# Two layers of a feed-forward network: the second one in six units of 1004 tokens, its second product two steps behind

## The chip, the cores and the metric

The kernel runs on one core of a Trainium2 chip. Its time is the device time of one execution in microseconds; three runs are shown, and one more execution was taken with the hardware profiler. Engines are called by the names of the profile: PE is TensorE (PEld its weight loads), ACT is ScalarE, DVE is VectorE, POOL is GpSimd, SP is the engine that issues most DMAs.

## The reference

```python
X = np.fft.fft(np.fft.fft(x, axis=1), axis=2).real      # x: 2 x 3008 x 256
x = X.reshape(6016, 256)
h = x @ w_in                                            # first layer, 256 -> 2048
g = where(h >= 1, h, where(h <= -1, 0, (h + 1)**2 / 4))
x = g @ w_out                                           # 2048 -> 256
h = x @ w2_in                                           # second layer, 256 -> 2048
g = maximum(0.01 * h, h)
out = g @ w2_out                                        # 2048 -> 256
```

All inputs and the output are float32 in value; the weights arrive as 64-bit words.

## The kernel before, in words

A first stage (up to about 75 us) makes the Fourier transform in the layout that the layers need, and folds part of it into the first layer's weights. Then come two layers, and the change is in the second. Tokens lie in the columns of a matmul. A layer handles its 6016 tokens in `NU` = 8 units of `UT` = 752, each unit as two halves of `H4` = 376 columns, and the 2048 hidden values as `NF` = 16 blocks of 128. One unit with one block is a step, so a layer has `N1` = 128 steps; the loop over `n` at the end of the function counts the steps of both layers.

Each operand of a matmul is held as a high part and a low part in a rounded float32 type (`FR`), and each product is made as high times high, high times low and low times high. A step of the second layer goes so:

- `first_2(u, f)` (L559): 12 matmuls on PE into `q`, one PSUM tile of two banks (pool `ps_ab`, two such tiles), two halves by two parts of the input by three products.
- L666, ACT writes `s` = 0.01 `q`; L667, DVE writes `s` = max(`q`, `s`).
- one step later `high` (L577): ACT rounds `s` into `gh`; `low` (L581): POOL writes `gl` = `s` - `gh`.
- `LAG` = 4 steps later `second` (L572): 12 matmuls of `gh`, `gl` with the output weights, into four PSUM accumulators `acc` (pool `ps_acc`, four tiles) that stay open for the 16 steps of a unit.
- after the sixteenth block `store` copies the accumulators out, two on ACT (L592) and two on DVE (L593); in the second layer SP then issues two DMAs to `out` (L596). In the first layer the copy is the input `yt[u]` of the second.

PE's order in a step is `first_2` of this step, then `second` of the step four before. Each engine runs its instructions in the order in which this loop issues them. `split_y` (L601 on ACT, L602 on DVE) splits a unit's input into `yh` some steps before the unit begins. The first layer's step (`layer_1`) has the same `high`, `low` and `second`, but only six matmuls in its first product and more elementwise work.

The tiles of both layers come from the same pools: `t3` (3 buffers each of `gh` and `gl`) and `t5` (5 buffers of the first result). Pools `ta`, `th` and `cp` on the right side serve the first layer alone. `jobs` is a list by step of work that is planned in by hand behind a step: the second layer's weights are read, turned to float32 and split from step `N1` - 6 on (`first_weights`, `second_weights`: a DMA, two ACT instructions, three DVE instructions, of which L217 and L222 read two operands from SBUF, and the split).

Of the kernel before, what the change touches and what calls it, by code (L numbers as in the profile page):

```python
# [19 lines left out]
P = 128  # L20
# [5 lines left out]
NU = NT // UT  # L26

# [130 lines left out]
def fnet_moe_kernel(ctx: ExitStack, tc: tile.TileContext, xpq, dft_e, dft_o, dft_d, sgn,  # L158
# [122 lines left out]
    with tc.manual_schedule():  # L281
# [249 lines left out]
        t3 = pool("t3", 3)  # L531
        t5 = pool("t5", 5)
        yp = [pool("yp0", 2)]
        only1 = ExitStack()
        ta = pool("ta", 2, only1, "right")
        th = pool("th", 3, only1, "right")

        N1 = NU * NF
        LAG = 4
# [12 lines left out]
        def first_2(u, f):  # L552
            p = psum_pair(f"q{u}_{f}")
            w, y = wa[f // 2][:, f % 2], yh[u]
            for t in range(2):
                a = 0
                for d in range(2):
                    for x, z in ((0, 0), (0, 1), (1, 0)):
                        T.matmul(p[:, t, :H4], lhsT=w[:, 2 * d + x, :], rhs=y[d][:, z, t, :],  # L559
                                 start=(a == 0), stop=(a == 5))  # L560
                        a += 1
            return p

        def second(n, f):
            if f == 0:
                for k in range(4):
                    acc[k] = psum_one(f"acc{n}_{k}")
            w, a, b = wb[f // 2][:, f % 2], gh.pop(n), gl.pop(n)
            for k in range(4):
                m, t = divmod(k, 2)  # L570
                for i, (x, y) in enumerate(((0, a), (0, b), (1, a))):
                    T.matmul(acc[k][:, :H4], lhsT=w[:, x, m * P:(m + 1) * P], rhs=y[:, t, :],  # L572
                             start=(f == 0 and i == 0), stop=(f == NF - 1 and i == 2))

        def high(n):
            gh[n] = t3.tile([P, 2, H4], FR, tag="gh", name="gh")
            A.copy(gh[n], gp[n])  # L577

        def low(n):
            gl[n] = t3.tile([P, 2, H4], FR, tag="gl", name="gl")  # L580
            G.tensor_tensor(out=gl[n], in0=gp.pop(n), in1=gh[n].bitcast(F32), op=ALU.subtract)  # L581

        def store(n, first):

            u = n % N1 // NF
            if first:
                yt[u] = by.tile([P, 2, 2, H4], F32, tag="by", name=f"y{u}")
                dst = [yt[u][:, m] for m in range(2)]
            else:
                dst = [to.tile([P, 2, H4], F32, tag="o", name=f"o{u}{m}") for m in range(2)]  # L590
            for t in range(2):
                A.copy(dst[0][:, t], acc[t][:, :H4])  # L592
                V.tensor_copy(dst[1][:, t], acc[2 + t][:, :H4])  # L593
            if not first:
                for m in range(2):
                    nc.sync.dma_start(out=out[m, :, u * UT:(u + 1) * UT],  # L596
                                      in_=dst[m].rearrange("p t n -> p (t n)"))

        def split_y(u, d):
            y = yp[u % 2].tile([P, 2, 2, H4], FR, tag="yh", name=f"yh{u}{d}")  # L600
            A.copy(y[:, 0], yt[u][:, d])  # L601
            V.tensor_tensor(out=y[:, 1], in0=yt[u][:, d], in1=y[:, 0].bitcast(F32), op=ALU.subtract)  # L602
            yh.setdefault(u, {})[d] = y
# [16 lines left out]
        for j in range(8):  # L620
            plan_at(20 + 12 * j, *zip((0, 2, 3, 6, 9), w3s[j]))
            plan_at(N1 - 6 + 2 * j, *zip((0, 3, 3), w3s[j][5:]))
            plan_at(N1 - 3 + 2 * j, *zip((0, 1, 2, 2, 3, 4, 4), w4s[j]))
        for d in range(2):
            plan_at(N1 - 26 + 6 * d, (0, lambda d=d: split_y(0, d)))
        for u in range(1, NU):
            plan(N1 + NF * (u - 1) + 8, [lambda u=u: split_y(u, 0)])
            plan(N1 + NF * (u - 1) + 11, [lambda u=u: split_y(u, 1)])

        def layer_1(n):  # L630
# [26 lines left out]
            if new:  # L657
                A.activation(r, r, AF.Square, scale=0.5 / 15.5, bias=0.5)  # L658
                sums(n)

        def layer_2(n):
            if n < 2 * N1:
                u, f = divmod(n - N1, NF)
                p = first_2(u, f)[:, :, :H4]
                gp[n] = g = t5.tile([P, 2, H4], F32, tag="r", name="s")
                A.activation(g, p, AF.Copy, scale=0.01)  # L666
                V.tensor_tensor(out=g, in0=p, in1=g, op=ALU.max)  # L667
            if N1 <= n - 1 < 2 * N1:
                high(n - 1)
                low(n - 1)  # L670
            sums(n)

        def sums(n):
            m = n - LAG
            if m >= 0:
                second(m, m % NF)
                if m % NF == NF - 1:
                    store(m, m < N1)

        for n in range(2 * N1 + LAG):  # L680
            if n < N1:
                layer_1(n)
            else:
                if n < N1 + 2:
                    layer_1(n)
                if n == N1 + 1:
                    only1.close()
                    right.close()
                    yp.append(pool("yp1", 2))
                    to = pool("to", 2)  # L690
                layer_2(n)
            for job in jobs.get(n, ()):
# [49 lines left out]
```

## Time and profile before

| | |
|---|---|
| three runs | 1040.7, 1040.75, 1043.45 us; median 1040.75 |
| the profiled execution | 1040.43 us, span 1038.7 us, so 1.73 us lie outside the span |
| granted TensorE clock, mean over the span | 0.993 |
| PE busy, PEld busy | 1004.1 us (97%), 971.7 us (94%) |
| DVE, ACT, POOL busy | 619.7 us, 624.1 us, 495.6 us |
| first matmul of the second layer | 499.25 us into the span |

A matmul's busy time is longer than the distance to the next one's start, since matmuls overlap; distances between starts are what the text below uses. A granted clock of 1.00 is 2.4 GHz. In a timeline row, "x12" merges twelve like instructions, and the brackets say how long the engine was idle before the row and what released it.

### The profile page before, as it was taken

Reading aid. Unit: us, or ns where it says so; the run is one execution under the profiler, and the core shown is the slowest. Engines: PE = TensorE matmul, PEld = TensorE weight load, DVE = VectorE, ACT = ScalarE, POOL = GpSimd, SP = SyncE. Lnnn points to the kernel's source line nnn. Section 1 sums busy time; section 2 is a strip of 40 time slices with the busy share of each in tenths; the row PEclk is TensorE's granted clock in tenths of the full one; section 3 lists DMA queues with packets and bytes.
Section 4 is the critical chain, followed back from the end, with each engine's and each line's share of the span. In section 5 each row is a group of like instructions: output and inputs, shape, how many; then the busy total and the mean of one; then the engine's idle time right before and its main releaser. Section 6 shows DMA issues by size and latency. Waiting matters only on the chain.

```text
span 1038.7 us, 14411 instructions
## 1 busy us (share of the span) xinstructions
PE 1004.1 (97%) x5656; PEld 971.7 (94%) x5656; DVE 619.7 (60%) x912; ACT 624.1 (60%) x973; POOL 495.6 (48%) x274
## 2 busy tenths in 40 slices
PE   7996879999999999999999999999999999999998
PEld 5656779999999999999999999999999999999998
DVE  5978998898888888897898232232323223233221
ACT  4468678888888788878775444444444444344432
POOL 1004565655565565555644444444444444444443
PEclk9998999999999999999999999999999999999999
DMA  9921000000000000010220000000000000000000
GB/s 298 349 69 41 21 0 2 31 31 1 31 31 2 31 32 1 31 62 2 72 101 21 30 2 1 31 1 30 1 1 31 1 31 1 1 30 1 30 1 31
DMA packets 12164, 39.24 MB, mean 38 GB/s; under 512 B 1472, under 2 KB 1472, under 8 KB 11840
## 3 DMA queue, kind: packets, MB, share of 16 engines
q1 hardware_dynamic: 11232, 35.18, 9.4%
q0 software_dynamic: 864, 3.15, 1.7%
q8 instruction: 44, 0.72, 0.3%
q14 instruction: 24, 0.20, 0.1%
HBM read 30.06 MB, written 8.26 MB: 37 GB/s over the span
## 4 chain that ended last, share of the span: by engine, by line
PE 78%; DVE 9%; ACT 7%; issue 3%; DMA 2%; POOL 0%; DVEq 0%; ACTq 0%; POOLq 0%; SPq 0%
PE acc L572 43%; PE q L559 24%; PE p L548 9%; DVE r L654 2%; ACT gh L577 2%; DMA rw<-in_w_dram 2%; ACT r L658 1%; DVE cw L222 1%; DVE tw L217 1%; DVE aa L641 1%; ACT r L647 1%; DVE h L644 1%; ACT r L651 1%; PE do L442 1%; DMA x<-in_xpq_dram 1%
## 5 line engine op out<-in xcount | busy, mean ns | idle before, releaser
L581 POOL TENSOR_TENSOR gl<-s,gh 128x752 fp32r<-128x752 f32 x128 | 234.0, 1828 | 287.9 <-ACT gh L577 287.9
L581 POOL TENSOR_TENSOR gl<-r,gh 128x752 fp32r<-128x752 f32 x128 | 242.4, 1895 | 175.9 <-ACT gh L577 135.3
L667 DVE TENSOR_TENSOR s<-q,s 128x752 f32<-128x752 f32 x128 | 120.2, 939 | 301.4 <-ACT s L666 301.2
L572 PE MATMUL acc<-gh,wb 128*128 128x376 f32 x1024 | 282.4, 336 | 2.5 <-POOL wb L275 1.3
L559 PE MATMUL q<-yh,wc 128*128 128x376 f32 x1536 | 283.8, 333 | 0.0
L572 PE MATMUL acc<-gh,wd 128*128 128x376 f32 x1024 | 278.7, 333 | 0.6 <-DVE y L593 0.6
L559 PEld LDWEIGHTS q<-yh,wc 128*128 128x128 f32 x1536 | 265.0, 188 | 0.0
L577 ACT CAST gh<-s 128x752 fp32r<-128x752 f32 x128 | 105.1, 821 | 158.2 <-PE acc L572 155.1
L572 PEld LDWEIGHTS acc<-gh,wb 128*128 128x128 f32 x1024 | 187.1, 189 | 6.1 <-ACT r L651 1.8
L572 PEld LDWEIGHTS acc<-gh,wd 128*128 128x128 f32 x1024 | 186.1, 188 | 0.9 <-DVE y L593 0.9
L572 PE MATMUL acc<-gl,wb 128*128 128x376 f32 x512 | 172.6, 337 | 10.9 <-POOL gl L581 10.8
L666 ACT ACTIVATE s<-q 128x752 f32<-128x752 f32 x128 | 102.3, 799 | 124.9 <-PE q L559 124.9
L572 PE MATMUL acc<-gl,wd 128*128 128x376 f32 x512 | 170.5, 333 | 0.0
L548 PE MATMUL p<-bt,wa 127*128 127x376 f32 (+3 forms) x768 | 156.5, 340 | 8.0 <-DVE h L645 4.2
L548 PEld LDWEIGHTS p<-bt,wa 128*128 128x128 f32 (+1 forms) x768 | 136.5, 191 | 10.5 <-issue 5.0
L654 DVE TENSOR_TENSOR r<-h,r 128x752 f32<-128x752 f32 x128 | 129.3, 1010 | 4.5 <-ACT r L658 4.4
L572 PEld LDWEIGHTS acc<-gl,wb 128*128 128x128 f32 x512 | 96.6, 189 | 15.4 <-POOL gl L581 15.4
L647 ACT ACTIVATE r<-h 128x376 f32<-128x376 f32 x128 | 66.1, 517 | 73.7 <-DVE h L644 69.6
L658 ACT ACTIVATE r<-r 128x752 f32<-128x752 f32 x128 | 106.8, 834 | 4.1
L577 ACT CAST gh<-r 128x752 fp32r<-128x752 f32 x128 | 103.2, 806 | 0.1
L641 DVE SCALAR_TENSOR_TENSOR aa<-ct,g,p 128x376 f32<-128x376 f32 (+1 forms) x128 | 77.2, 603 | 41.0 <-PE p L548 40.7
L572 PEld LDWEIGHTS acc<-gl,wd 128*128 128x128 f32 x512 | 96.1, 188 | 0.0
(70 smaller groups left out, 650.6 us busy)
## 6 DMA issues: line engine op xcount, KB each, us to landing
rw<-in_w_dram SPq DMA_DIRECT2D x32, 512.0 KB, 3.7
out_dram<-o SPq DMA_DIRECT2D x16, 376.0 KB, 2.4
x<-in_xpq_dram SPq DMA_DIRECT2D x6, 512.0 KB, 6.4
x<-in_xpq_dram POOLq DMA_DIRECT2D x6, 512.0 KB, 7.7
me<-in_dft_e_dram SPq DMA_DIRECT2D x4, 567.0 KB, 16.0
mo<-in_dft_o_dram SPq DMA_DIRECT2D x2, 1128.0 KB, 19.8
w3f<-cw SPq DMA_DIRECT2D x8, 256.0 KB, 2.2
rf<-w3f SPq DMA_DIRECT2D x8, 256.0 KB, 2.6
```

Of the source, the lines that this page charges most:

```text
L217: V.scalar_tensor_tensor(out=self.tmp, in0=self.high, scalar=-0x80000000, in1=self.tmp, op0=ALU.bitwise_and, op1=ALU.bitwise_or)
L548: T.matmul(p[:, j, :n], lhsT=w[:m, 2 * j + x, :], rhs=b[:m, 2 * j + y, :n], start=(a == 0), stop=(a == 2))
L559: T.matmul(p[:, t, :H4], lhsT=w[:, 2 * d + x, :], rhs=y[d][:, z, t, :], start=(a == 0), stop=(a == 5))
L572: T.matmul(acc[k][:, :H4], lhsT=w[:, x, m * P:(m + 1) * P], rhs=y[:, t, :], start=(f == 0 and i == 0), stop=(f == NF - 1 and i == 2))
L577: A.copy(gh[n], gp[n])
L581: G.tensor_tensor(out=gl[n], in0=gp.pop(n), in1=gh[n].bitcast(F32), op=ALU.subtract)
L641: V.scalar_tensor_tensor(out=aa[:, :w], in0=ct[u][:, :w], scalar=g128[:, f:f + 1], in1=p[:, 0, :w], op0=ALU.mult, op1=ALU.add)
L647: A.activation(r[:, 0], h[:, 0], CLAMP, scale=15.5)
L654: V.tensor_tensor(out=g, in0=hp.pop(n - 1), in1=g, op=ALU.max)
L658: A.activation(r, r, AF.Square, scale=0.5 / 15.5, bias=0.5)
L666: A.activation(g, p, AF.Copy, scale=0.01)
L667: V.tensor_tensor(out=g, in0=p, in1=g, op=ALU.max)
```

## The change

The second layer is cut anew: `NV` = 6 units of two halves of `H6` = 502 columns (the last one of two halves of 498), so 96 steps instead of 128. Its matmuls are as many in a step as before, each over 502 columns. The second layer has its own tiles, `s` (3 buffers, pool `ts`), `gh2` and `gl2` (2 buffers each, pool `g2`); they lie where the first layer's pools were, which are closed at the seam between the layers. `th` has 2 buffers instead of 3. The second product runs 4 steps behind in the first layer, 3 for its last two steps, and 2 in the second layer; `sums` issues what is due, which at two steps of the seam is two products. At step `N1` both drain steps of the first layer are issued together. `split_y` joins pieces of two or three of the first layer's units, and the jobs that prepare the second layer's output weights begin one step earlier.

```diff
--- before.py
+++ after.py
@@ -24,6 +24,8 @@
 NF = DFF // P
 UT = 2 * H4
 NU = NT // UT
+NV = 6
+H6 = 502
 
 
 
@@ -528,15 +530,16 @@
         late.close()
 
 
-        t3 = pool("t3", 3)
-        t5 = pool("t5", 5)
         yp = [pool("yp0", 2)]
         only1 = ExitStack()
-        ta = pool("ta", 2, only1, "right")
-        th = pool("th", 3, only1, "right")
+        t3 = pool("t3", 3, only1)
+        t5 = pool("t5", 5, only1)
+        drain1 = ExitStack()
+        ta = pool("ta", 2, drain1, "right")
+        th = pool("th", 2, drain1, "right")
 
         N1 = NU * NF
-        LAG = 4
+        N2 = N1 + NV * NF
         gh, gl, acc, yh, hp, rp, gp = {}, {}, {}, {}, {}, {}, {}
 
         def first_1(u, f):
@@ -549,58 +552,80 @@
                              start=(a == 0), stop=(a == 2))
             return p
 
-        def first_2(u, f):
-            p = psum_pair(f"q{u}_{f}")
-            w, y = wa[f // 2][:, f % 2], yh[u]
+        def half(v):
+
+            return min(H6, NT // 2 - H6 * v)
+
+        def halves(t, n):
+            return t[:, :2 * n].rearrange("p (t n) -> p t n", t=2)
+
+        def first_2(v, f):
+            p = psum_pair(f"q{v}_{f}")
+            w, y, n = wa[f // 2][:, f % 2], yh[v], half(v)
             for t in range(2):
                 a = 0
                 for d in range(2):
                     for x, z in ((0, 0), (0, 1), (1, 0)):
-                        T.matmul(p[:, t, :H4], lhsT=w[:, 2 * d + x, :], rhs=y[d][:, z, t, :],
+                        T.matmul(p[:, t, :n], lhsT=w[:, 2 * d + x, :], rhs=y[d][:, z, t * n:(t + 1) * n],
                                  start=(a == 0), stop=(a == 5))
                         a += 1
-            return p
-
-        def second(n, f):
+            return p[:, :, :n]
+
+        def second(m, f, n):
             if f == 0:
                 for k in range(4):
-                    acc[k] = psum_one(f"acc{n}_{k}")
-            w, a, b = wb[f // 2][:, f % 2], gh.pop(n), gl.pop(n)
+                    acc[k] = psum_one(f"acc{m}_{k}")
+            w, a, b = wb[f // 2][:, f % 2], gh.pop(m), gl.pop(m)
             for k in range(4):
-                m, t = divmod(k, 2)
+                r, t = divmod(k, 2)
                 for i, (x, y) in enumerate(((0, a), (0, b), (1, a))):
-                    T.matmul(acc[k][:, :H4], lhsT=w[:, x, m * P:(m + 1) * P], rhs=y[:, t, :],
+                    T.matmul(acc[k][:, :n], lhsT=w[:, x, r * P:(r + 1) * P], rhs=y[:, t, :],
                              start=(f == 0 and i == 0), stop=(f == NF - 1 and i == 2))
 
-        def high(n):
-            gh[n] = t3.tile([P, 2, H4], FR, tag="gh", name="gh")
-            A.copy(gh[n], gp[n])
-
-        def low(n):
-            gl[n] = t3.tile([P, 2, H4], FR, tag="gl", name="gl")
-            G.tensor_tensor(out=gl[n], in0=gp.pop(n), in1=gh[n].bitcast(F32), op=ALU.subtract)
-
-        def store(n, first):
-
-            u = n % N1 // NF
-            if first:
-                yt[u] = by.tile([P, 2, 2, H4], F32, tag="by", name=f"y{u}")
-                dst = [yt[u][:, m] for m in range(2)]
-            else:
-                dst = [to.tile([P, 2, H4], F32, tag="o", name=f"o{u}{m}") for m in range(2)]
+        def parts_of(m):
+
+            if m < N1:
+                return (t3.tile([P, 2, H4], FR, tag=tag, name=tag) for tag in ("gh", "gl"))
+            n = half((m - N1) // NF)
+            return (halves(g2.tile([P, 2 * H6], FR, tag=tag, name=tag), n) for tag in ("gh2", "gl2"))
+
+        def high(m):
+            gh[m], gl[m] = parts_of(m)
+            A.copy(gh[m], gp[m])
+
+        def low(m):
+            G.tensor_tensor(out=gl[m], in0=gp.pop(m), in1=gh[m].bitcast(F32), op=ALU.subtract)
+
+        def store_1(u):
+
+            yt[u] = by.tile([P, 2, 2 * H4], F32, tag="by", name=f"y{u}")
             for t in range(2):
-                A.copy(dst[0][:, t], acc[t][:, :H4])
-                V.tensor_copy(dst[1][:, t], acc[2 + t][:, :H4])
-            if not first:
-                for m in range(2):
-                    nc.sync.dma_start(out=out[m, :, u * UT:(u + 1) * UT],
-                                      in_=dst[m].rearrange("p t n -> p (t n)"))
-
-        def split_y(u, d):
-            y = yp[u % 2].tile([P, 2, 2, H4], FR, tag="yh", name=f"yh{u}{d}")
-            A.copy(y[:, 0], yt[u][:, d])
-            V.tensor_tensor(out=y[:, 1], in0=yt[u][:, d], in1=y[:, 0].bitcast(F32), op=ALU.subtract)
-            yh.setdefault(u, {})[d] = y
+                A.copy(yt[u][:, 0, t * H4:(t + 1) * H4], acc[t][:, :H4])
+                V.tensor_copy(yt[u][:, 1, t * H4:(t + 1) * H4], acc[2 + t][:, :H4])
+
+        def store_2(v):
+            n = half(v)
+            dst = [to.tile([P, 2 * H6], F32, tag="o", name=f"o{v}{m}") for m in range(2)]
+            for t in range(2):
+                A.copy(dst[0][:, t * n:(t + 1) * n], acc[t][:, :n])
+                V.tensor_copy(dst[1][:, t * n:(t + 1) * n], acc[2 + t][:, :n])
+            for m in range(2):
+                nc.sync.dma_start(out=out[m, :, 2 * H6 * v:2 * H6 * v + 2 * n], in_=dst[m][:, :2 * n])
+
+        def split_y(v, d):
+
+
+            y = yp[v % 2].tile([P, 2, 2 * H6], FR, tag="yh", name=f"yh{v}{d}")
+            begin, end = 2 * H6 * v, 2 * H6 * v + 2 * half(v)
+            pieces = []
+            for u in range(begin // UT, (end - 1) // UT + 1):
+                lo, hi = max(begin, UT * u), min(end, UT * (u + 1))
+                pieces.append((y[:, :, lo - begin:hi - begin], yt[u][:, d, lo - UT * u:hi - UT * u]))
+            for o, i in pieces:
+                A.copy(o[:, 0], i)
+            for o, i in pieces:
+                V.tensor_tensor(out=o[:, 1], in0=i, in1=o[:, 0].bitcast(F32), op=ALU.subtract)
+            yh.setdefault(v, {})[d] = y
 
         jobs = {}
 
@@ -620,12 +645,12 @@
         for j in range(8):
             plan_at(20 + 12 * j, *zip((0, 2, 3, 6, 9), w3s[j]))
             plan_at(N1 - 6 + 2 * j, *zip((0, 3, 3), w3s[j][5:]))
-            plan_at(N1 - 3 + 2 * j, *zip((0, 1, 2, 2, 3, 4, 4), w4s[j]))
+            plan_at(N1 - 4 + 2 * j, *zip((0, 1, 2, 2, 3, 4, 4), w4s[j]))
         for d in range(2):
             plan_at(N1 - 26 + 6 * d, (0, lambda d=d: split_y(0, d)))
-        for u in range(1, NU):
-            plan(N1 + NF * (u - 1) + 8, [lambda u=u: split_y(u, 0)])
-            plan(N1 + NF * (u - 1) + 11, [lambda u=u: split_y(u, 1)])
+        for v in range(1, NV):
+            for d in range(2):
+                plan_at(N1 + NF * (v - 1) + 8 + 3 * d, (0, lambda v=v, d=d: split_y(v, d)))
 
         def layer_1(n):
 
@@ -656,39 +681,51 @@
                 low(n - 2)
             if new:
                 A.activation(r, r, AF.Square, scale=0.5 / 15.5, bias=0.5)
-                sums(n)
 
         def layer_2(n):
-            if n < 2 * N1:
-                u, f = divmod(n - N1, NF)
-                p = first_2(u, f)[:, :, :H4]
-                gp[n] = g = t5.tile([P, 2, H4], F32, tag="r", name="s")
+            if n < N2:
+                v, f = divmod(n - N1, NF)
+                p = first_2(v, f)
+                gp[n] = g = halves(ts.tile([P, 2 * H6], F32, tag="s", name="s"), half(v))
                 A.activation(g, p, AF.Copy, scale=0.01)
                 V.tensor_tensor(out=g, in0=p, in1=g, op=ALU.max)
-            if N1 <= n - 1 < 2 * N1:
+            if N1 <= n - 1 < N2:
                 high(n - 1)
                 low(n - 1)
-            sums(n)
+
+        def lag(m):
+
+            return 4 if m < N1 - 2 else 3 if m < N1 else 2
+
+        done = 0
 
         def sums(n):
-            m = n - LAG
-            if m >= 0:
-                second(m, m % NF)
-                if m % NF == NF - 1:
-                    store(m, m < N1)
-
-        for n in range(2 * N1 + LAG):
+            nonlocal done
+            while done < N2 and done + lag(done) <= n:
+                m, first = done, done < N1
+                i, f = divmod(m if first else m - N1, NF)
+                second(m, f, H4 if first else half(i))
+                if f == NF - 1:
+                    (store_1 if first else store_2)(i)
+                done += 1
+
+        for n in range(N2 + 2):
             if n < N1:
                 layer_1(n)
             else:
-                if n < N1 + 2:
-                    layer_1(n)
+                if n == N1:
+                    layer_1(N1)
+                    layer_1(N1 + 1)
+                    drain1.close()
+                    right.close()
+                    to = pool("to", 2, side="right")
+                    ts = pool("ts", 3, side="right")
                 if n == N1 + 1:
                     only1.close()
-                    right.close()
                     yp.append(pool("yp1", 2))
-                    to = pool("to", 2)
+                    g2 = pool("g2", 2)
                 layer_2(n)
+            sums(n)
             for job in jobs.get(n, ()):
                 job()
 
```

## Rows read from the trace of the kernel before

**Rows 1.** The page: span, busy time, shares of the chain that ended last.

```profile
span 1038.7 us, 14411 instructions
...
PE 1004.1 (97%) x5656; PEld 971.7 (94%) x5656; DVE 619.7 (60%) x912; ACT 624.1 (60%) x973; POOL 495.6 (48%) x274
...
PE 78%; DVE 9%; ACT 7%; issue 3%; DMA 2%; POOL 0%; DVEq 0%; ACTq 0%; POOLq 0%; SPq 0%
```

**Rows 2.** Windows: us, busy time (instructions) by engine, clock, DMA share, GB/s.

```profile
530.00:1030.00 500.00, 500.00 (x2921) 500.00 (x2920) 170.09 (x175) 221.05 (x290) 222.66 (x123) 1.00 0.04 16
```

**Rows 3.** The chain in order of time: start us, us, engine, tile, line.

```profile
543.40 2.07 PE acc L572 x12
...
1012.07 2.07 PE acc L572 x12
```

**Rows 4.** Timeline, second layer: start us, us, engine, line, operation, [idle before].

```profile
701.52 2.21 PE L559 MATMUL q<-yh,wc 128*128 128x376 f32 x12
701.77 0.82 ACT L577 CAST gh<-s 128x752 fp32r<-128x752 f32 x1 [1.28 <-PE acc L572]
702.66 1.80 POOL L581 TENSOR_TENSOR gl<-s,gh 128x752 fp32r<-128x752 f32 x1 [2.29 <-ACT gh L577]
...
703.58 0.34 PE L572 MATMUL acc<-gh,wd 128*128 128x376 f32 x1
...
703.77 0.80 ACT L666 ACTIVATE s<-q 128x752 f32<-128x752 f32 x1 [1.19 <-PE q L559]
...
705.64 2.22 PE L559 MATMUL q<-yh,wc 128*128 128x376 f32 x12
```

**Rows 5.** Timeline of TensorE, first stage: one-column and plain float32 matmuls.

```profile
37.85 0.95 PE L340 MATMUL g<-sg,cw 128*128 128x1 f32 x8
38.66 4.34 PE L442 MATMUL do<-mo,xt 126*127 126x376 f32 x20
...
72.51 0.80 PE L409 MATMUL ds<-me,xt 126*127 126x376 f32 x2
73.14 4.16 PE L442 MATMUL co<-mo,col 126*128 126x376 f32 x16
```

**Rows 6.** Lines by form: busy us, mean ns of one | idle before.

```profile
L667 DVE TENSOR_TENSOR s<-q,s 128x752 f32<-128x752 f32 x128 | 120.2, 939 | 301.4 <-ACT s L666 301.2
...
L602 DVE TENSOR_TENSOR yh<-y,yh 128x752 fp32r<-128x752 f32 x16 | 27.0, 1689 | 25.8 <-ACT yh L601 25.8
...
L593 DVE COPY o<-acc 128x376 f32<-128x376 f32 x16 | 8.0, 541 | 8.0 <-PE acc L572 8.0
...
L592 ACT COPY o<-acc 128x376 f32<-128x376 f32 x16 | 6.8, 472 | 3.8 <-PE acc L572 3.8
```

**Rows 7.** Waits of 530 to 1030 us: waited for, us in total, times, longest.

```profile
ACT gh L577 <- PE acc L572: 152.0, 117, 1.3
```

**Rows 8.** Timeline between the layers: TensorE, then VectorE, then GpSimd.

```profile
499.25 2.22 PE L559 MATMUL q<-yh,wc 128*128 128x376 f32 x12
...
515.68 2.21 PE L559 MATMUL q<-yh,wc 128*128 128x376 f32 x12
518.48 0.44 PE L572 MATMUL acc<-gh,wd 128*128 128x376 f32 x1 [0.58 <-DVE y L593]
...
514.21 2.19 DVE L217 SCALAR_TENSOR_TENSOR tw<-rw,tw 128x512 int32<-128x512 int32 x1
516.43 0.69 DVE L222 SCALAR_TENSOR_TENSOR cw<-rw,tw 128x512 int32<-128x512 int32 x1
...
514.03 1.81 POOL L581 TENSOR_TENSOR gl<-s,gh 128x752 fp32r<-128x752 f32 x1 [2.31 <-ACT gh L577]
```

**Rows 9.** Timeline, the end of the run.

```profile
1034.24 1.07 DVE L593 COPY o<-acc 128x376 f32<-128x376 f32 x2 [7.96 <-PE acc L572]
1034.38 0.33 PE L572 MATMUL acc<-gh,wd 128*128 128x376 f32 x1
```

**Rows 10.** DMA issues of 1000 to 1039 us: KB each, median us to landing.

```profile
out_dram<-o SPq DMA_DIRECT2D x2, 376.0 KB, 2.3
```

## The prediction

> **What bounds the kernel now.** I read the page first: PE is busy for 97% of the span and holds 78% of the chain that ended last, no other engine more than 9% [rows 1]. Busy time of overlapping matmuls proves little, so the windows come next: in 500 us of the second layer PE is never idle, at a granted clock of 1.00, while DVE, ACT and POOL are busy for 170, 221 and 223 us [rows 2]. There the time is the number of matmuls times the distance between their starts. For that distance I take two starts of `acc` far apart in the chain [rows 3]: 1012.07 - 543.40 = 468.67 us. One step, from `q` to `q`, is 705.64 - 701.52 = 4.12 us [rows 4], so these are 114 steps of 4.111 us, and with 24 matmuls in a step the distance is 171.3 ns. At 2.4 GHz 376 columns take 156.7 ns; 14.6 ns are something else. The reading closes: from the first matmul of the layer, 499.25 [rows 8], to the last, 1034.38 [rows 9], lie 3,072 matmuls and the first layer's last 48: 3,120 x 0.1713 = 534.5 us, and with the one stall named below 535.2, against 535.3 read.
>
> **The matmuls: what the 14.6 ns are.** The change makes 2,304 matmuls of the second layer's 3,072, with the same columns in sum (1,920 over 502, 384 over 498). So it gains only what is paid for each matmul rather than for each column. No row shows the rounded type at a width that differs enough, so I bound it.
> - Lower end, all of it goes with the columns: 0.4556 ns for each, 228.7 and 226.9 ns, sum 526.2 us as before. Gain 0.
> - Upper end, columns run at 2.4 GHz with a small fixed part and something else holds the distance at 376 columns. The nearest row for a small fixed part is the plain float32 matmul: (73.14 - 72.51) / 2 = 315 ns, which is 376 columns twice at 2.4 GHz (313 ns) and 2 ns [rows 5]. Then 502 columns take 211.2 and 498 take 209.5 ns, 485.9 us in all. Gain 40.
> - Between them, 14.6 ns fixed: 209.2 + 14.6 = 223.8 ns and 207.5 + 14.6 = 222.1 ns; 1,920 x 0.2238 + 384 x 0.2221 = 515.0 us against 3,072 x 0.1713 = 526.2. Gain 11.2.
>
> I take 11.2. The upper end needs something that takes 171 ns whatever the columns, the weight load first of all; but eight one-column matmuls, each with its own load, take 38.66 - 37.85 = 0.81 us, 0.10 us each [rows 5]. Against the lower end: the plain matmul adds next to nothing to its columns, so columns as such do pass at the clock; it streams them at half the rate, though, so this is a hint and no proof.
>
> The Trainium skill ("TensorE: Matmul & The Clock Gate", section Back-to-back issue gap) gives the isolated distance at full clock as columns / 2.4 and 2.5 ns. By that 376 columns would be 159.2 ns; rows 3 measure 171.3, so the measurement decides, and the rule leaves 12.1 ns of each matmul unexplained. If the rule's fixed part is nevertheless all there is and these 12.1 ns go with the columns, the layer would take 524.3 us.
>
> **The second product two steps behind.** Its 24 matmuls per step need `gl` in time. Count from the start of `second` that follows `first_2(n)`. ACT begins `s` 703.77 - 703.58 = 0.19 us after it [rows 4]. ACT takes 472 ns for 376 columns [rows 6] and 0.80 for 752, so 0.87 ns for each more: `s` over 1004 takes 1.02, `gh` 0.82 + 0.22 = 1.04. Today `gh` waits until PE has finished reading its buffer, 152.0 us in sum [rows 7]. With two buffers the reader is the product three steps back, which lag 2 has issued before `first_2(n)`, so no such wait is left. POOL begins 0.07 us after `gh` (701.77 + 0.82, 702.66) and takes 1.80 for 752 columns [rows 4]; in proportion 2.41 for 1004, which is the most that it can be if it has a fixed part, and 1.80 the least. Sum 0.19 + 1.02 + 0.03 + 1.04 + 0.07 + 2.41 = 4.76 us. PE reaches that product 24 matmuls later, 5.37 us. It is 0.6 us early: cost nothing. PE covers it; if the chain is late by d, each step that waits gives the next one its wait as a start, so 96 steps cost about 96 x d / 2. DVE's max is off this chain: it is needed one step later.
>
> ACT, POOL and DVE per step stay below PE: 2.06, 2.41 and about 1.2 of 5.37 us. In the first sixteen steps the weights are prepared as well. There L217 takes 2.19 us when POOL's `gl` starts before it and ends at 515.84, and L222 0.69 right after [rows 8]: these DVE instructions wait for POOL. They are queued behind the max on DVE and in front of the next one, 4 us later; nothing of the `gl` chain is behind them. ACT's weight instructions are issued behind `gh`. With longer steps both have more room than before. Cost 0, up to 2 if they delay POOL.
>
> **The seam.** Today PE stands once: `q` at 515.68 should be done after 12 x 0.1713, at 517.74, but `acc` starts at 518.48, waiting for DVE's copies [rows 8], which are late behind L217: 0.74 us. In the change the second layer's first product follows the first layer's last one with no `first_2` between them, and needs the accumulators copied. ACT must first do `s` and `gh` (0.19 + 1.02 + 1.04) and then a copy of 0.47: 2.7 us after the start of that product, which itself takes 12 x 0.1713 = 2.06. Some 0.7 us of waiting takes the place of 0.74. Bounds: nothing if the copies come first, 3 us if DVE is again behind L217 with two instructions. The weight jobs one step earlier put two such instructions into the last step of the first layer; their cover is that layer's lag of four. The release of `gh2`'s memory waits for products that PE runs before `second` needs it. Net 0.
>
> **The first layer.** `split_y` of unit 0 now handles 1004 columns in two pieces instead of 752 in one; one takes DVE 1.69 us today [rows 6], so 0.6 more each, twice, in a layer where DVE has little room. I take 0.5 us, bounds 0 and 2. `th` with two buffers costs nothing: the last reader of the older one stands ahead of the new writer on DVE itself. Tiles at other addresses: nothing known, put into the range.
>
> **The end.** After the last `first_2` DVE's max is on the chain: 0.19 + 1.02 + 0.1 + 1.21 (939 ns for 752 and 541 for 376 make 1.06 for each column [rows 6]) + 0.05 + 1.04 + 0.07 + 2.41 = 6.1 us to `gl`, while two products of 2.67 us and one matmul cover 5.55: PE stands 0.55 us, where lag 4 covered it. DVE's last copies are 1.07 us for two of 376 columns [rows 9]; the last of them grows by 0.13. The two stores are 498 KB each instead of 376, which land in 2.3 us [rows 10]: in proportion 0.7 more. Together 1.4.
>
> **Sum**, against the profiled execution: 1040.43 - 11.2 + 0.5 + 1.4 = 1031.1 us. The median of the runs shown is 0.3 above that execution, so about 1031.
>
> **The rivals.**
> 1. The overhead goes with the columns but for the 2 ns of rows 5: (171.3 - 2) / 376 = 0.4503 ns, 228.0 and 226.2 ns, 524.7 us; gain 1.5, and with 1.9 of costs 1040.8. For it: the rounded type reads its columns at twice the pace of the plain one, and a limit on that pace would be a cost for each column; against it: such a limit would have to lie just under the clock. The rule of the Trainium skill named above, taken this way, gives 1040.4.
> 2. The slower side: `gh` waits for PE after all. If the buffer comes free only with the product two steps back, which ends 2.69 us after the count begins, the chain is 2.69 + 0.25 + 1.04 + 0.07 + 2.41 = 6.46 us, 1.09 more than 5.37, and 96 x 1.09 / 2 = 52 us are lost: about 1083. It decides from a lateness of 0.26 us on (0.26 / 2 x 96 = 12.5 us, the gain and 0.3%). For it: today ACT does wait for PE there [rows 7], and buffers are fewer; against it: the order of the loop, and 0.6 us of reserve.
> 3. Columns alone: the upper end, 1040.4 - 40.3 + 1.9 = 1002. Speaks against it the 0.10 us of a weight load.
>
> **Chances.** Forecast 0.61, rival 1 0.20, rival 2 and other stalls of its kind 0.12, rival 3 0.07. The forecast's own range is 1026 to 1035: addresses and costs above, 1.5 ns either way on 2,304 matmuls being 3.5 us. The range 1025 to 1041 takes in rival 1 and leaves out rivals 2 and 3. Faster by over 0.3% (3.1 us, about what a measurement can tell from no change): the forecast, rival 3 and a little of rival 1, 0.68. Within 0.3%: most of rival 1, 0.19. Slower 0.13.
>
> **What would show it.** In the profile after, the distance between starts in a step of the last layer: 223.8 ns is right, 228 is rival 1, 211 rival 3. PE without idle time through the layer, no PE or PEld wait for `gl`; ACT's wait for PE at `gh` gone; POOL at 2.4 us; 0.5 us of PE standing before the last product. The prediction is wrong if POOL takes well over 3 us for 1004 columns, or if a stall appears at each unit's start, where the accumulators are copied.

## The result, and the profile after

The changed kernel takes 1053.21 us (median of four runs, 1051.27 to 1055.43) against 1040.95 us: ratio 1.0113, interval 1.0082 to 1.0144. It is slower by 1.1%; the forecast was 1031 us and faster, with 0.13 for slower. The four runs lie in two pairs, near 1051.3 and 1055.2 us, and the profiled execution, 1055.43 us, is one of the longer pair: its span exceeds the one before by more than the medians differ. One execution of e11 below took 1106.33 us at a mean granted clock of 0.845 and is left out of the time given there.

The page of the changed kernel, its span and three of its groups (busy us, mean ns of one | idle before), beside [rows 1, 6]:

```profile
span 1053.6 us, 12688 instructions
...
L597 POOL TENSOR_TENSOR gl<-s,gh 128x1004 fp32r<-128x1004 f32 (+1 forms) x96 | 225.7, 2351 | 304.7 <-ACT gh L594 289.0
...
L690 ACT ACTIVATE s<-q 128x1004 f32<-128x1004 f32 (+1 forms) x96 | 96.7, 1008 | 306.2 <-PE q L569 306.2
...
L594 ACT CAST gh<-s 128x1004 fp32r<-128x1004 f32 (+1 forms) x96 | 98.1, 1022 | 6.0 <-issue 5.2
```

The single instructions cost what was forecast: POOL's `gl` 2.35 us (2.41), `s` 1.01 (1.02), `gh` 1.02 (1.04). ACT's wait for PE ahead of `gh`, 152 us before [rows 7], is gone. What is not there is a shorter matmul. The chain in order of time, two first products of the second layer far apart, as in [rows 3]:

```profile
560.96 2.75 PE q L569 x12
...
933.27 2.75 PE q L569 x12
```

These are 372.31 us and 68 steps of 5.475 us, 228.1 ns for a matmul (forecast 223.8, rival 1 228.0). The last unit's 498 columns take 225.4 ns, so the layer's matmuls need 524.6 us where they needed 526.2: a gain of 1.6 us instead of 11.2. The windows of the seam (us, busy time of PE, PEld, DVE, ACT, POOL, then the granted clock) say where the rest went:

```profile
510.00:520.00 10.00, 7.89 (x34) 6.79 (x33) 7.38 (x9) 4.34 (x6) 3.03 (x2) 0.85 0.24 79
520.00:530.00 10.00, 4.54 (x19) 3.29 (x17) 6.25 (x4) 5.93 (x10) 4.68 (x2) 0.84 0.20 61
530.00:540.00 10.00, 9.80 (x35) 8.03 (x36) 4.07 (x6) 2.54 (x4) 1.51 (x1) 0.80 0.05 19
```

PE is busy for 4.5 of 10 us at the worst, and the clock is granted in part at its lower level, 1.2 GHz. The timeline names the waits: PE, then DVE, then ACT.

```profile
515.85 4.42 PE L569 MATMUL q<-yh,wc 128*128 128x502 f32 x12 [2.11 <-DVE s L691]
...
526.28 0.49 PE L582 MATMUL acc<-gh,wd 128*128 128x502 f32 x1 [3.80 <-ACT y L603]
...
530.20 0.79 PE L582 MATMUL acc<-gh,wd 128*128 128x502 f32 x1 [1.86 <-DVE y L604]
...
507.35 2.20 DVE L224 SCALAR_TENSOR_TENSOR cw<-rw,tw 128x512 int32<-128x512 int32 x1
509.47 2.40 DVE L262 TENSOR_TENSOR wc<-rf,wc 128x256 fp32r<-128x256 f32 x2
511.79 0.93 DVE L679 TENSOR_TENSOR r<-h,r 128x752 f32<-128x752 f32 x1
...
512.83 0.82 ACT L594 CAST gh<-r 128x752 fp32r<-128x752 f32 x1 [3.49 <-DVE r L679]
...
522.39 1.03 ACT L594 CAST gh<-s 128x1004 fp32r<-128x1004 f32 x1 [5.19 <-issue]
...
525.75 0.85 ACT L603 COPY y<-acc 128x376 f32<-128x376 f32 x2
```

Read it from the top of each cause. DVE is held by the weight jobs L224 (2.20 us) and L262 (2.40) before it makes the last `r` of the first layer at 511.79; ACT stands 3.49 us for it, the max that frees `q`'s buffer comes late, and PE stands 2.11 us ahead of the third first product. Then ACT stands 5.19 us ahead of the first `gh` of the second layer and begins it at 522.39, just when PE ends the first layer's last product: its last matmul on a `gl` runs from 521.97 to 522.31. Behind it in ACT's queue are `s`, the next `gh` and the copies of the accumulators (525.75), so PE stands 3.80 us for ACT and 1.86 for DVE, which has two weight jobs (L262, 4.82 us from 523.75 on) and a max in front of its copies. The three windows lack 0.15, 0.16 and 0.20 of the full clock, 5.1 us; at half the clock, the lower level, that is 10.2 of the 30 us.

The account of the two spans, 15.0 us before rounding. The matmul row is their number times their distance; the first layer's last 48 matmuls, 8.2 us in both kernels, stand in no row; the seam is what is left.

| stretch | before | after | difference |
|---|---|---|---|
| first stage, to the first matmul of layer 1 | 77.2 | 79.1 | +1.9 |
| layer 1, to the first matmul of layer 2 | 422.0 | 422.8 | +0.8 |
| matmuls of layer 2 | 526.2 | 524.6 | -1.6 |
| seam, standing and lower clock | 0.7 | 12.2 | +11.5 |
| PE standing before the last products | 0 | 1.7 | +1.7 |
| from the last matmul's start to the end | 4.3 | 5.0 | +0.7 |

Of the seam's 12.2 us the three stands are 7.8; the other 4.4 are left for the lower clock.

The change does not touch the first stage; in the profiles of the kernels below it ends between 76.9 and 78.6 us, so those 1.9 us are not counted on it.

### The profile page after: what moved, and what is told of

Its sections match the earlier page's. It is cut to its first block, busy times and chain, and to the rows that moved or that the text cites. A ratio compares the mean times of both kernels' runs of the same rounds, so it can differ in the third digit from the quotient of the medians.

```text
span 1053.6 us, 12688 instructions
## 1 busy us (share of the span) xinstructions
PE 1009.4 (96%) x4888; PEld 884.3 (84%) x4888; DVE 629.9 (60%) x886; ACT 603.1 (57%) x915; POOL 486.0 (46%) x242
## 4 chain that ended last, share of the span: by engine, by line
PE 77%; DVE 10%; ACT 7%; issue 3%; DMA 1%; POOL 1%; SPq 0%; ACTq 0%; DVEq 0%; POOLq 0%
PE acc L582 42%; PE q L569 24%; PE p L551 9%; ACT gh L594 2%; DVE r L679 2%; ACT r L683 2%; DVE cw L224 1%; DVE aa L666 1%; DMA rw<-in_w_dram 1%; DVE tw L219 1%; ACT r L672 1%; DVE h L669 1%; ACT r L676 1%; PE g L337 1%; PE do L444 1%
## 5 line engine op out<-in xcount | busy, mean ns | idle before, releaser
L597 POOL TENSOR_TENSOR gl<-s,gh 128x1004 fp32r<-128x1004 f32 (+1 forms) x96 | 225.7, 2351 | 304.7 <-ACT gh L594 289.0
L691 DVE TENSOR_TENSOR s<-q,s 128x1004 f32<-128x1004 f32 (+1 forms) x96 | 115.4, 1202 | 324.6 <-ACT s L690 324.6
L569 PE MATMUL q<-yh,wc 128*128 128x502 f32 (+1 forms) x1152 | 279.6, 392 | 2.1 <-DVE s L691 2.1
L690 ACT ACTIVATE s<-q 128x1004 f32<-128x1004 f32 (+1 forms) x96 | 96.7, 1008 | 306.2 <-PE q L569 306.2
L582 PE MATMUL acc<-gh,wd 128*128 128x502 f32 (+1 forms) x768 | 253.7, 391 | 5.7 <-ACT y L603 3.8
L569 PEld LDWEIGHTS q<-yh,wc 128*128 128x128 f32 x1152 | 218.3, 190 | 48.0 <-DVE s L691 2.4
L582 PE MATMUL acc<-gl,wb 128*128 128x376 f32 x512 | 172.7, 337 | 12.3 <-POOL gl L597 12.3
L582 PEld LDWEIGHTS acc<-gh,wd 128*128 128x128 f32 x768 | 145.3, 189 | 36.8 <-ACT y L603 4.1
L582 PE MATMUL acc<-gl,wd 128*128 128x502 f32 (+1 forms) x384 | 150.8, 393 | 1.6 <-POOL gl L597 1.6
L551 PEld LDWEIGHTS p<-bt,wa 128*128 128x128 f32 (+1 forms) x768 | 136.1, 191 | 10.6 <-issue 4.6
L594 ACT CAST gh<-s 128x1004 fp32r<-128x1004 f32 (+1 forms) x96 | 98.1, 1022 | 6.0 <-issue 5.2
L582 PEld LDWEIGHTS acc<-gl,wd 128*128 128x128 f32 x384 | 72.9, 190 | 17.0 <-POOL gl L597 2.0
```

Source lines behind the costliest of these rows:

```text
L551: T.matmul(p[:, j, :n], lhsT=w[:m, 2 * j + x, :], rhs=b[:m, 2 * j + y, :n], start=(a == 0), stop=(a == 2))
L569: T.matmul(p[:, t, :n], lhsT=w[:, 2 * d + x, :], rhs=y[d][:, z, t * n:(t + 1) * n], start=(a == 0), stop=(a == 5))
L582: T.matmul(acc[k][:, :n], lhsT=w[:, x, r * P:(r + 1) * P], rhs=y[:, t, :], start=(f == 0 and i == 0), stop=(f == NF - 1 and i == 2))
L594: A.copy(gh[m], gp[m])
L597: G.tensor_tensor(out=gl[m], in0=gp.pop(m), in1=gh[m].bitcast(F32), op=ALU.subtract)
```

## The experiments

Two questions were open: what a matmul of the rounded type costs, and which part of the change makes the seam. All ratios are to the kernel before, run beside it on the same chip.

**e1 and e5: what a matmul costs by itself.** Rows of 60 like matmuls (`REP` = 60), every operand ready, each row once in one profiled execution.

```python
p = ps.tile([P, 512], F32, tag="p", name=name)
for i in range(REP):
    T.matmul(p[:m, :n], lhsT=wt[k][:, i % 8, :m], rhs=mov[k][:, o:o + n], start=True, stop=True)
```

> This kernel leaves out the whole computation: it runs rows of 60 matmuls, each with its own weight load, at several widths and in three types, and nothing else on TensorE. Theory C (the distance between two matmuls of the rounded float32 type goes with the columns): 0.449 ns for each column and 2 ns, so 117 ns at 256 columns, 171 at 376, 199 at 440, 227 to 228 at 502, 232 at 512; weights of 64 columns instead of 128 change nothing; bfloat16 at 376 and 502 columns runs at the clock, 159 and 212 ns. Rival F (a toll of 14.6 ns for each matmul, 209.2 + 14.6 at 502): 121, 171, 198, 224, 228 ns, and with weights of 64 columns less, if the weight load is the toll.

> Leaves out the whole computation, as the first of these kernels: rows of 60 matmuls with their own weight loads, more widths and several start columns of the moving operand. Theory A (a fixed toll of 13.3 ns, 32 columns' worth, and up to some 6 ns more where the moving operand does not begin and end on whole 64-byte lines): 120, 147, 173, 213 ns at 256, 320, 384, 480 columns, 200 at 448, 227 at 512, all with start 0; about 223 at 502 with start 0, 228 and more with starts of 2 or 6 columns; 512 with start 2 or 6 clearly over 227. Rival C (goes with the columns): 0.4556 ns a column, 204 at 448, 219 at 480, 229 at 502, 233 at 512, whatever the start. bfloat16 at 212 ns for 502 columns whatever the start.

The timeline of PE in e5 (start us, us of the whole row); the start of the row after it less its own start, divided by 60, is the distance. Rows `ri`, `rl`, `rm`, `rn`, `ro` and `rp` begin at column 0, 2, 4, 6, 8 and 16 of the moving tile; `rk` and `rq` at 0 and 2.

```profile
19.57 7.36 PE L44 MATMUL ra<-movr,wtr 128*128 128x256 f32 x60
26.76 8.96 PE L44 MATMUL rb<-movr,wtr 128*128 128x320 f32 x60
...
107.36 13.56 PE L44 MATMUL ri<-movr,wtr 128*128 128x502 f32 x60
120.76 13.78 PE L44 MATMUL rj<-movr,wtr 128*128 128x504 f32 x60
134.38 13.79 PE L44 MATMUL rk<-movr,wtr 128*128 128x512 f32 x60
148.00 13.57 PE L44 MATMUL rl<-movr,wtr 128*128 128x502 f32 x60
161.41 13.90 PE L44 MATMUL rm<-movr,wtr 128*128 128x502 f32 x60
175.15 13.83 PE L44 MATMUL rn<-movr,wtr 128*128 128x502 f32 x60
188.81 13.84 PE L44 MATMUL ro<-movr,wtr 128*128 128x502 f32 x60
202.49 13.78 PE L44 MATMUL rp<-movr,wtr 128*128 128x502 f32 x60
216.11 14.18 PE L44 MATMUL rq<-movr,wtr 128*128 128x512 f32 x60
...
268.50 12.87 PE L44 MATMUL bu<-movb,wtb 128*128 128x502 bf16 x60
281.21 12.89 PE L44 MATMUL bv<-movb,wtb 128*128 128x502 bf16 x60
```

All rows of e5 that begin at column 0, with what stands beyond columns / 2.4 GHz:

| columns | 256 | 320 | 376 | 384 | 440 | 448 | 480 | 498 | 502 | 504 | 512 |
|---|---|---|---|---|---|---|---|---|---|---|---|
| distance, ns | 119.8 | 146.7 | 173.5 | 173.3 | 199.8 | 206.7 | 216.7 | 226.7 | 223.3 | 227.0 | 227.0 |
| beyond the columns, ns | 13.2 | 13.3 | 16.8 | 13.3 | 16.5 | 20.0 | 16.7 | 19.2 | 14.2 | 17.0 | 13.7 |

From 256 to 512 columns the distance grows by 0.419 ns for each, which is the full clock (0.417). So the toll for each matmul is real, about the 14.6 of the forecast, and rival 1's mechanism (the overhead goes with the columns: 117 and 232 ns at 256 and 512) is out. But the toll is not one number: at the same start it is 13.2 to 20.0 ns by the width, in no order that these rows explain. And it changes with the start: 502 columns take 223.3, 223.5, 229.0, 227.7, 228.0 ns as the start column moves from 0 to 8, and 512 take 233.5 from column 2. In bfloat16 502 columns take 211.8 ns.

In e1 a weight tile of 64 columns instead of 128 took 376 columns from 173.3 to 170.2 ns and 502 from 223.5 to 233.0, so the toll is not simply the length of the weight load. At 128 and 192 columns e1 has 110.8 and 112.2 ns: something does hold the distance there, but at 111 ns, not at the 171 of rival 3. Theory A's 64-byte lines fail in part: 448 columns take 206.7 where 200 were expected, and 502 from column 16, on a 64-byte line, take 227.0.

**e9: the place of one operand relative to the other.** The same rows with the weights' start moved too (`a = s + P * (i % c)`, `lhsT=wt["r"][:, a:a + P]`).

> Leaves out the whole computation: rows of 60 matmuls of 512 (then 448 and 384) columns, where the moving operand and the weights start at several columns of their tiles; both tiles begin at 128 modulo 256 bytes. Theory R (the extra toll comes from the address of the moving operand relative to that of the weights, modulo 256 bytes): 226.7 ns where both are shifted alike (8, 16, 32 columns) and at shifts of 64, 128, 192, 256 columns; 232 to 234 at shifts of 2, 8, 16, 32, 48, 96 columns of one alone, whichever of the two is shifted. Rival L (the moving operand's own 64-byte lines): 226.7 at every moving start that is a multiple of 16 columns and whatever the start of the weights, more only at 2 and 8.

PE in e9, of 512 columns but for the last three rows. Start columns of moving operand and weights: `ra` 0, 0; `rb` 2, 0; `rc` 8, 0; `rd` 16, 0; `rg` 64, 0; `rl` 0, 8; `ro` 0, 48; `rp` 0, 64; `rq` 8, 8; `rv` and `rx` 0, 0; `rw` 32, 0.

```profile
18.60 13.79 PE L48 MATMUL ra<-movr,wtr 128*128 128x512 f32 x60
32.22 14.17 PE L48 MATMUL rb<-movr,wtr 128*128 128x512 f32 x60
46.23 14.16 PE L48 MATMUL rc<-movr,wtr 128*128 128x512 f32 x60
60.23 13.89 PE L48 MATMUL rd<-movr,wtr 128*128 128x512 f32 x60
73.96 14.10 PE L48 MATMUL re<-movr,wtr 128*128 128x512 f32 x60
...
101.89 13.80 PE L48 MATMUL rg<-movr,wtr 128*128 128x512 f32 x60
115.53 14.15 PE L48 MATMUL rh<-movr,wtr 128*128 128x512 f32 x60
...
170.34 14.15 PE L48 MATMUL rl<-movr,wtr 128*128 128x512 f32 x60
184.33 14.16 PE L48 MATMUL rm<-movr,wtr 128*128 128x512 f32 x60
...
212.28 13.90 PE L48 MATMUL ro<-movr,wtr 128*128 128x512 f32 x60
226.01 13.77 PE L48 MATMUL rp<-movr,wtr 128*128 128x512 f32 x60
239.62 13.80 PE L48 MATMUL rq<-movr,wtr 128*128 128x512 f32 x60
253.26 13.79 PE L48 MATMUL rr<-movr,wtr 128*128 128x512 f32 x60
...
308.13 12.55 PE L48 MATMUL rv<-movr,wtr 128*128 128x448 f32 x60
320.51 12.39 PE L48 MATMUL rw<-movr,wtr 128*128 128x448 f32 x60
332.75 10.57 PE L48 MATMUL rx<-movr,wtr 128*128 128x384 f32 x60
```

227.0 ns at equal starts; 233.5 and 233.3 when the moving operand is shifted by 2 or 8 columns, 233.2 when the weights are shifted by 8 instead; 227.3 again when both are shifted by 8. 64 columns, 256 bytes, of one alone change nothing (227.3 and 226.8). And 16 columns of the moving operand cost the same, 228.8, as 48 of the weights: -48 is 16 modulo 64 columns. At 512 columns theory R holds and rival L does not; R's 232 at 16 columns was too high. The other two widths were measured at 0 and at 32 columns of the moving operand: 384 take 173.3 and about 176 ns, as R has it, but 448 take 206.3 at equal starts and only 204.0 shifted, so there the equal place is the dearer one. So in this type a matmul of 512 columns takes 226.7 to 233.5 ns by where its operands lie relative to each other modulo 256 bytes. Why, no run shows.

**e2, e3, e4: the seam.** e2 puts a gap before the second layer's pool, e3 puts the weight jobs back, e4 does both. The pools explain the gap: `t3`'s six buffers are 18,048 bytes, and `yp1`, put in their place, 16,064; so `g2`, which follows it, begins 1,984 bytes before the end of `t3`, on the buffer that by the program's addresses holds the last `gl` of the first layer. So the first `gh2` may be written only when PE has read that `gl`.

```diff
                     yp.append(pool("yp1", 2))
+                    pool("gap", 1).tile([P, 496], F32, name="gap")
                     g2 = pool("g2", 2)
...
-            plan_at(N1 - 4 + 2 * j, *zip((0, 1, 2, 2, 3, 4, 4), w4s[j]))
+            plan_at(N1 - 3 + 2 * j, *zip((0, 1, 2, 2, 3, 4, 4), w4s[j]))
```

> The changed kernel with the second layer's gh2 moved up by 1984 bytes in SBUF, so that its first buffer no longer overlaps the last gl of the first layer. Theory M (the seam is lost to that overlap: gh of step N1 waits for the first layer's last product, and ACT's queue stands behind it): the 5.19 us ACT wait goes, PE's 3.80 and 1.86 us of standing at the accumulators fall to under 1, no half clock after 525 us; 6 to 9 us faster than the changed kernel, 1044 to 1047. Rival J (the weight jobs that were put one step earlier are the first cause, through DVE's queue): PE's stand of 2.1 us before the third first product stays, and the time falls by 2 us at most.

> The changed kernel with the weight jobs at the steps where they were before the change (one step later). Theory M: the overlap stays and so do most of the losses; PE's 2.1 us stand before the third first product goes, 2 to 4 us faster than the changed kernel, 1049 to 1051. Rival J: most of the loss goes, 6 us or more, 1047 or less.

> Both of the two edits. Theory M with J as the smaller part: the seam is nearly clean, PE stands under 1.5 us there, granted clock 1.00 throughout the second layer; 1041 to 1044. If a third thing (the order of the first layer's two drain steps, or the two products back to back) holds the seam, more than 3 us of standing stay, 1045 or more.

e2: 1046.78 us, ratio 1.0058 (1.0043 to 1.0073). e3: 1049.43 us, 1.0086 (1.0070 to 1.0101). e4: 1042.63 us, 1.0017 (1.0007 to 1.0026). PE's waits at the seam, first in e2:

```profile
514.73 4.56 PE L569 MATMUL q<-yh,wc 128*128 128x502 f32 x12 [2.12 <-DVE s L691]
...
521.67 0.49 PE L582 MATMUL acc<-gh,wd 128*128 128x502 f32 x1 [0.33 <-ACT y L603]
```

in e3 PE, then ACT ahead of the first `gh` of the second layer:

```profile
522.77 0.79 PE L582 MATMUL acc<-gh,wd 128*128 128x502 f32 x1 [5.53 <-ACT y L603]
...
517.15 1.03 ACT L594 CAST gh<-s 128x1004 fp32r<-128x1004 f32 x1 [7.46 <-PE acc L582]
```

in e4:

```profile
517.42 0.50 PE L582 MATMUL acc<-gh,wd 128*128 128x502 f32 x1 [0.33 <-ACT y L603]
```

Each edit removes the stand that its theory named and no other: the gap leaves the 2.12 us ahead of `q`, the old jobs leave 5.53 us ahead of `acc`, both together leave 0.33. In e3 the profile names the wait of `gh` outright: 7.46 us for PE's product. The gap also moves `gh2` and `gl2` by 192 modulo 256 bytes, but a step of 502 columns takes 5.47 us in the change and in e2, so the 6.4 us are not that. Theory M (6 to 9 us) gives 6.4, J's part 3.8, together 10.6 of the 12.3 us that the change lost; the clock stays at 1.00 through the second layer in e4. In e4's profile the spans differ by 2.1 us from before: +0.8 in the first layer and +2.4 at the end, about -1.4 in the matmuls, the rest in the first stage and the seam.

**e6, e7, e8: the columns and their place.** e6 is the changed kernel with `H6` = 512 (and 448 in the last unit) and nothing else; e8 is that with both seam edits; e7 keeps 502 columns with both seam edits, but begins each half at a multiple of 512 columns.

```diff
-            return t[:, :2 * n].rearrange("p (t n) -> p t n", t=2)
+            return t.rearrange("p (t n) -> p t n", t=2)[:, :, :n]
...
-                        T.matmul(p[:, t, :n], lhsT=w[:, 2 * d + x, :], rhs=y[d][:, z, t * n:(t + 1) * n],
+                        T.matmul(p[:, t, :n], lhsT=w[:, 2 * d + x, :], rhs=y[d][:, z, t * 512:t * 512 + n],
```

> The changed kernel with one number changed: halves of 512 columns (five units of 1024 tokens and one of 896, as 2 x 448) instead of 502, so that each half begins and ends on a 64-byte line; everything else, the overlap at the seam too, stays. Theory A: 1,920 x 0.2267 + 384 x 0.200 = 512.1 us for the layer's matmuls instead of 524.6, so 12 us less than the changed kernel, 1039 to 1042. Rival C: nothing, 1051 to 1055.

> The kernel with both seam edits, halves of 502 columns as in the change, but each half begins at a multiple of 512 columns in its tile, so only the start is aligned and not the width. If the start makes the extra toll: 223.4 ns a matmul, 10 us less than with both seam edits alone, 1031 to 1034. If the width makes it: 228 stays, 1041 to 1044.

> Halves of 512 and 448 columns and both seam edits (the buffer moved off the first layer's last gl, the weight jobs at their old steps). Theory A: 1042.6 - 12.5 = 1029 to 1032, about 1% faster than the kernel before. Rival C: 1041 to 1044.

e6: 1040.77 us, ratio 1.0001 (0.9992 to 1.0011): one number takes back 12.4 us, and the seam is as bad as in the change. e7: 1038.3 us, 0.9974 (0.9965 to 0.9983). e8: 1037.97 us, 0.9974 (0.9963 to 0.9984). Both missed their bands by 4 to 6 us. The timeline of PE in e8 shows which matmuls:

```profile
702.21 2.90 PE L569 MATMUL q<-yh,wc 128*128 128x512 f32 x12
704.95 0.40 PE L582 MATMUL acc<-gh,wd 128*128 128x512 f32 x1
...
707.74 2.90 PE L569 MATMUL q<-yh,wc 128*128 128x512 f32 x12
```

`q`'s twelve take 704.95 - 702.21 = 2.74 us, 228 ns, but `acc`'s 2.79, 232.5. In e6 they were equal, 226.7. By the program's addresses the gap of e8 had moved `gh2` and `gl2` from 192 to 64 modulo 256 bytes, while weights and `yh` stand at 192. That led to e9 above, and to the next two.

**e10, e12: the same place for all.** The gap is 128 bytes larger (`[P, 448]` for `[P, 416]`), in e8 and in e7.

> The version with halves of 512 columns and both seam edits, with gh2 and gl2 128 bytes further up in SBUF, so that they stand at 192 modulo 256 bytes as the weights do (there at 64). Theory R: acc's distance 227 instead of 232.5 ns, 960 x 5.5 ns = 5.3 us less, 1032 to 1034. Rival L: no change, 1037 to 1039.

> Halves of 502 columns that begin at multiples of 512 columns in their tiles, both seam edits, and gh2 and gl2 at 192 modulo 256 bytes like the weights (there at 64). Theory R (the toll depends on the place of the moving operand relative to the weights): acc falls from 227.5 to about 224.3 ns, as q is, and the kernel by 960 x 3.3 ns = 3 us against the version without this place, to 1034 to 1036. If 502 columns as such cost 228 ns, no change, 1037.5 to 1039.

e10: 1030.59 us, ratio 0.9904 (0.9890 to 0.9917). e12: 1033.78 us, 0.9931 (0.9918 to 0.9945). PE in e10:

```profile
700.12 2.88 PE L569 MATMUL q<-yh,wc 128*128 128x512 f32 x12
702.84 0.39 PE L582 MATMUL acc<-gh,wd 128*128 128x512 f32 x1
...
705.56 2.88 PE L569 MATMUL q<-yh,wc 128*128 128x512 f32 x12
```

Now both products take 2.72 us, 226.7 ns. 128 bytes are worth 7.4 us to e8 and 4.5 to e7, more than expected; both kernels came out below their bands, by 1.4 and 0.2 us. The reason is that the first products grew shorter too, though their own operands did not move: from e8 to e10 a matmul of `acc` by 6.0 ns (e9 has 5.3 for that shift) and one of `q` by 1.2, a step from 5.53 to 5.44 us, 6.9 us over 80 steps; from e7 to e12 a step falls from 5.42 to 5.36 us, 4.8 us. What is left lies in scatter and the last unit. With e12 at 223.3 ns for all matmuls of 502 columns, that width is no fault in itself; the packing at 2,008 bytes and the places of the buffers are.

**e11: the end.** In e10 the last two `gl` are made by DVE.

```diff
-            G.tensor_tensor(out=gl[m], in0=gp.pop(m), in1=gh[m].bitcast(F32), op=ALU.subtract)
+            (G if m < N2 - 2 else V).tensor_tensor(out=gl[m], in0=gp.pop(m), in1=gh[m].bitcast(F32), op=ALU.subtract)
```

> The same, and the last two gl are made by DVE, which is idle there, instead of POOL. If the end stands because two products run without a first product between them and POOL's 2.3 us are in the chain (PE stands 1.8 us there in the version before): the stand falls to about 0.7 us, 1 us less than the kernel above. If the end is set by the copies and stores, no change.

PE's wait before the last products, in e10 and then in e11:

```profile
1019.76 0.19 PEld L582 LDWEIGHTS acc<-gl,wd 128*128 128x128 f32 x1 [1.86 <-POOL gl L597]
```

```profile
1017.92 0.19 PEld L582 LDWEIGHTS acc<-gl,wd 128*128 128x128 f32 x1 [0.93 <-DVE gl L597]
```

The stand is halved, 1.86 to 0.93 us, about as expected (0.7). The time is 1029.61 us (median of four), ratio 0.9902 (0.9887 to 0.9918); against e10 that is within the intervals, so of the 0.9 us only the stand is shown.

## Why the prediction was wrong

**What bounds the kernel** was right: outside the seam and the end PE never waits in the changed layer, and every microsecond there is a distance between matmuls.

**The matmuls** are the first step that failed, in its size: the term "14.6 ns fixed" gave a gain of 11.2 us, and 1.6 was measured. It was right in kind (e5: a toll for each matmul, 13.2 to 20.0 ns), and a gain of that size is to be had: in e10 the layer's matmuls need 1,920 x 226.7 + 384 x 202.9 ns = 513.2 us (202.9 from a step of 448 columns, 966.83 to 971.70, between 24 matmuls), 13.0 less than before. But I took the toll of one width in one packing and carried it to another width and another packing as a constant. The change's halves start 2,008 bytes apart, 216 modulo 256, and by the program's addresses its buffers lie at several places modulo 256; it paid 228.1 ns instead of 223.8, and 225.4 instead of 222.1 in the last unit: 9.6 us, nearly the whole gain. e12, the same 502 columns at equal places, takes 223.3, so the place is the cause and not the width. Rival 1 forecast 228.0 for another reason, which e5 refutes; that it agrees is luck. I had named "Tiles at other addresses" and given them a part of 3.5 us of range; they were worth nearly three times that. What in the engine makes the toll, and why it differs from width to width, stays open: 448 columns take 206.3 ns in e9 and 202.9 in e10, both at equal places, and the kernel before has 171.3 at 376 columns where e5's row at equal places has 173.5.

One reading of [rows 5] was wrong. A plain float32 matmul leaves two entries in the trace: e5's row of 60 such matmuls has 120, 421 ns apart at 502 columns. So the 0.63 us from 72.51 to 73.14 are one matmul, 376 columns four times and some 3 ns, and the eight one-column entries are four matmuls. The plain type streams its columns at a quarter of the rounded type's rate, not at half. The fixed part stays small, so neither the three sums nor the choice between them hung on it.

The Trainium skill ("TensorE: Matmul & The Clock Gate", section Back-to-back issue gap) gives columns / 2.4 and 2.5 ns. e5 agrees for bfloat16, 211.8 ns at 502 columns; the rounded float32 type is 11 to 18 ns above it, and there the measurement decides. The Trainium skill ("TensorE: Matmul & The Clock Gate", section Step-by-step: what each phase is for) says that the weight load has a read port of its own and takes no read bandwidth from the running matmul. e9 measures that the place of the weights relative to the moving operand is worth up to 6.7 ns of 227; whether that goes through a port, no run shows.

**The second product two steps behind** was right in the steady layer: no wait for `gl`, no wait of ACT for PE. Rival 2 did not occur there.

**The seam** is the step that made the change slower: "Net 0", with bounds of nothing and 3 us, against 11.5. Two sentences of it failed. "The release of `gh2`'s memory waits for products that PE runs before `second` needs it" is true of the order on PE and missed who stands behind the waiting `gh`: ACT's whole queue, and with it the accumulators' copies (e2: 6.4 us). "their cover is that layer's lag of four" missed that the jobs stand ahead of the last max on DVE, which ACT's drain and then `q`'s buffer wait for (e3: 3.8 us). Neither sentence counted the lower clock in the windows of such stands, some 4.4 us. The wait of the two products back to back was foreseen at 0.7 us, and e4 shows it: PE stands 0.33 us.

**The first layer** was forecast at 0.5 us and measured 0.8. **The end** was forecast at 1.4 and is 2.4: the stores and copies took 0.7 of their 0.85, but PE stood 1.7 us longer, not 0.55, because already the last but one product has no first product in front of it, and needs its `gl` 2.7 us after the count begins, where 4.76 are needed. e11 shows that POOL's share of that chain is in it.

## What to carry to other kernels

Before resizing tiles of a matmul, measure one matmul at the new size and at the new places of both operands; a distance taken from the old layout is not a constant of the engine. When tiles move into memory that was another stage's, look up which buffer lies under the first new one, who reads it last, and everything that stands behind the waiting instruction on its engine. One version here (e10), halves of 512 columns with the buffers at equal places and the seam mended, is 1% faster than the kernel before, while the same idea packed otherwise was 1% slower.

## What the runs showed of the hardware

- A matmul of the rounded float32 type costs its columns at the full clock and 13.2 to 20.0 ns more by the width, from 256 columns on (e5, start 0: 119.8 ns at 256 columns, 206.7 at 448, 227.0 at 512), in bfloat16 at 502 columns only 2.6 ns more (211.8).
- At 512 columns it costs up to 6.5 ns beyond that, by the difference of the two operands' addresses modulo 256 bytes (e9): 227.0 at 0, 228.8 at 64, 232.3 at 128, 233.2 at 192, 233.3 at 32. At 448 columns it is the other way: 206.3 at 0 and 204.0 at 128.
- In the three windows of 10 us in which PE stood 2.1, 3.8 and 1.9 us the granted clock was 0.85, 0.84 and 0.80. In e4, where PE stood 0.33 us at the seam, it was 1.00 throughout the second layer.
